# Newton step ahead of a division, two operands on GpSimd, and two more load buffers in a fused attention and feed-forward kernel

## The chip, the core and the metric

The kernel runs on one core of a Trainium2 chip. A core has a matmul engine (TensorE, PE in the profile, whose weight loads are listed apart as PEld), three engines for elementwise work (VectorE or DVE, ScalarE or ACT, GpSimd or POOL) and SyncE (SP), which issues most transfers. Each engine works through its own instructions in the order in which the program gives them, and waits on semaphores for the others. TensorE and ScalarE reach both memories on the chip, SBUF and PSUM; matmul results land in PSUM, and GpSimd does not read them here. The metric is the device time of one execution in microseconds (us); lower is better.

## What is computed

Attention with normalised q and k over 8 batches, 12 heads, 448 positions and 64 features, and behind it a feed-forward block with a softmax-weighted activation and a layer norm. All is float32.

```python
def rmsnorm(x, g):
    return x / np.sqrt(np.mean(x * x, axis=-1, keepdims=True) + 1e-06) * g
scores = scale * np.matmul(rmsnorm(q, g_q), rmsnorm(k, g_k).transpose(0, 1, 3, 2))
attn = np.exp(scores - np.max(scores, axis=-1, keepdims=True))
attn = attn / (np.sum(attn, axis=-1, keepdims=True) + 1e-09)
x = np.matmul(attn, v)                  # brought to (3584, 768)
...
h = x @ w_in                            # (3584, 1024)
e = np.exp(h - np.max(h, axis=-1, keepdims=True))
solu = h * e / (np.sum(e, axis=-1, keepdims=True) + 1e-09)
ln = (solu - mu) / np.sqrt(var + 1e-06) * g_ln
out = ln @ w_out                        # (3584, 768)
```

## The kernel before

Only `fast_path` runs with these inputs. The order of instructions on each engine is written out by hand; three stages follow each other.

**Stage 1, attention** (to about 331 us). A pair n is two heads of one batch; a quad m is two pairs, a = 2m and b = 2m + 1; there are 24 quads. For a pair, `load` (L627) brings q and k in eight transfers on SP's queue (L634) into one tile of the ring `qk`; `squares` (L653, ScalarE), `row_sums` (L660, DVE), `fold_sums` (L668, GpSimd, for a whole quad) and then `rsqrt_seed` (L690, ScalarE: a logarithm and an exponential) and `rsqrt_step` (L697, DVE: one Newton step of four instructions, L701 to L704) make the inverse root of the mean square; `normalise` (L706, GpSimd) multiplies, `qk_transpose` (L720, DVE) turns the result, and `gain` (L725, ScalarE) scales it. This work is for the next quad but one (squares, sums) and the next quad (the rest). For the quad itself `scores` (L804) and `scores_last` make the score blocks on PE and their exponentials E on ScalarE (L802), three PSUM buffers in turn; `add` (L836, DVE) adds two blocks of E into es; `outputs` and `values` (L846, L859) multiply with v into two PSUM banks o, one for each pair; `sums` (L870) adds up E and es on PE. `inverse` (L889) turns those sums round, takes reciprocals (DVE) and copies them between partitions (GpSimd, L903); `divide` (L905) is four DVE instructions (twice L910, L911) that multiply the two banks o by the reciprocals into xo, and so free the banks for the next quad's values; `store_x` (L914) sends xo to DRAM on SP's queue.

`unit` runs one piece and then whatever `later` has put off until then. After quad m's sums, `later(1, divide(m))` makes the division fall due right after the first score block of quad m + 1, ahead of the Newton step for quad m + 2, which in quads 2 and 3 is called after the second and the first score block (L1451 to L1455). SP's order within a quad is: v for the next quad (L647, two more transfers at L651), the store of the quad before, eight q,k transfers for pair a + 6, eight for pair b + 6, and in some quads a piece of w_in (L510).

**Stage 2, first matmul** (to about 585 us). PE multiplies x with w_in in 14 groups of two row tiles by a scheme of seven products instead of eight. A finished tile t goes through `ff_max`, `ff_exp` (ScalarE), `ff_mult` (L1055, a DVE multiply of 128x1024), `ff_moments` (L1059: DVE statistics, and on GpSimd a power, L1071, and a shift, L1073), `ff_norm` (L1075, ScalarE) and `ff_spread` (L1084, a DVE transpose and four stores on SP). The table `waits` in `in_parts` (L1094) says how many units after the tile these five fall due. The last group's tiles are 26 and 27; tile 27 is finished one product ahead of tile 26 and has the key (NG - 1, 1).

**Stage 3, second matmul.** Seven blocks n of four row tiles each, seven products P1 to P7 a block, and seven matmul groups (a "slot" each) a product. `load_u` (L1130) brings the spread tiles back into a ring of six buffers ur (SP, L1133). `make` (L1146) forms the seven operands: a11, a12 and a22 are ScalarE copies (L1151 to L1155), s1, s2, s3, s4 are DVE instructions of 128x512 (L1157 to L1163); s3 of block 0 reads a11 and ur, s4 reads a12 and s2. `inner_sums` (L1165) makes four sums of each operand on GpSimd (L1174 to L1177, 128x256). In `outer_product` (L1179) each slot's result is taken from its PSUM bank by ScalarE or DVE (L1208, L1210, L1235, L1248, L1258), and the next matmul group into that bank waits for this. At the end of `fast_path`, `made(n, name, ...)` puts an operand's two halves behind the slots named; inner sums of a product stand six slots ahead of it. Block 1's loads are put at slots 10, 11, 15 to 18, 21 and 22, its a11 at slots 18 and 21.

Of the kernel before, what the change touches and what calls it, by code (L numbers as in the profile page):

```python
# [9 lines left out]
FP32 = mybir.dt.float32  # L10
# [4 lines left out]
OP = AluOpType  # L15
# [351 lines left out]
def fast_path(  # L367
# [24 lines left out]
    nc = tc.nc  # L392
    B, H, S, D = q.shape
    DM, DFF = moe_w_in.shape
    P = 128
    NJ = S // P
    NB = S // 32
# [6 lines left out]
    NG = NT // 2  # L404
# [14 lines left out]
    loads = first.enter_context(tc.tile_pool(name="loads", bufs=2))  # L419
# [207 lines left out]
    def load(n):  # L627
        b, hp = divmod(n, NP)
        h0 = 2 * hp
        d = st[n] = {}  # L630
        d["qk"] = loads.tile([P, 2, NB, 32], FP32, tag="qk", name="qk", bufs=5)
        for s, src in enumerate((q, k)):
            for g in range(4):
                nc.sync.dma_start(  # L634
                    d["qk"][g * 32 : g * 32 + 32, s],
                    src[b, h0 + g // 2].rearrange("(b t) (x d) -> x t b d", t=32, x=2)[g % 2],
                )
# [162 lines left out]
    def exponentials(d, kc, s):  # L800
        d["E", kc] = big_tile("E")[:, 0 : 2 * S].rearrange("p (h t) -> p h t", h=2)
        nc.scalar.activation(d["E", kc], s[:, :, 0:S], AF.Exp)  # L802

    def scores(n, kc):  # L804
        d = st[n]
        s = ps_t.tile([P, 2, 512], FP32, tag="t", name="s")

        for c in range(0, P, D):
            for h in range(2):
                hh = slice(h * D, (h + 1) * D)  # L810
                keys = slice(NJ * c + kc, NJ * (c + D - 1) + kc + 1, NJ)
                nc.tensor.matmul(  # L812
                    s[c : c + D, h, 0:S], d["qkT"][hh, 1, keys], d["qkT"][hh, 0, :],
                    start=True, stop=True,
                )
        exponentials(d, kc, s)
# [88 lines left out]
    def divide(m):  # L905
        xo = quads[m]["xo"] = work.tile([P, 2, S], FP32, tag="xo", name="xo", bufs=1)
        for i in range(2):
            n = 2 * m + i
            r = work.tile([P, NB, 32], FP32, tag="r", name="r", bufs=1)
            nc.vector.transpose(r, quads[m]["rc"][:, i].rearrange("p t b -> p (t b) ()").to_broadcast([P, NB, 32]))  # L910
            nc.vector.tensor_tensor(xo[:, i], st[n]["o"], r.rearrange("d b i -> d (b i)"), OP.mult)  # L911
            del st[n]

    def store_x(m):  # L914
        b, hp = divmod(2 * m, NP)
        nc.sync.dma_start(
            xd[b].rearrange("(c p) t -> p c t", p=P)[:, hp : hp + 2], quads.pop(m)["xo"]
        )
# [7 lines left out]
    def load_x(g):  # L926
        x = gs[g, "x"] = xs.tile([P, KD, 2 * P], FP32, tag="x", name="xg")
        t = 2 * g * P
        while t < 2 * (g + 1) * P:
            b, c = divmod(t, S)  # L930
            n = min(S - c, 2 * (g + 1) * P - t)
            o = t - 2 * g * P

            (nc.sync if g < 2 else nc.scalar).dma_start(x[:, :, o : o + n], xd[b].rearrange("(c p) t -> p c t", p=P)[:, :, c : c + n])
            t += n

    def sizes(g):

        x = gs[g, "x"].rearrange("p c t -> p (c t)")
        n = HD * 2 * P  # L940
        sm = gs[g, "s"] = xs.tile([P, 3, HD, P], FP32, tag="x", name="xsum")
        for i in range(2):
            nc.scalar.activation(
                sm.rearrange("p k c t -> p (k c t)")[:, 0:n], x[:, i * n : (i + 1) * n], AF.Square,
                accum_out=xmax[:, 2 * g + i : 2 * g + i + 1],
            )
# [7 lines left out]
    def block_sums(g, part):  # L954

        if part == 0:
            gs[g, "A"] = x_blocks(g)
        a11, a12, a21, a22 = gs[g, "A"]
        sm = gs[g, "s"]
        s1, s2, s4 = [sm[:, i] for i in range(3)]  # L960
        if part == 0:
            nc.gpsimd.tensor_tensor(s1, a21, a22, OP.add)
            nc.gpsimd.tensor_tensor(s2, s1, a11, OP.subtract)
        else:
            nc.gpsimd.tensor_tensor(a21, a11, a21, OP.subtract)
            nc.gpsimd.tensor_tensor(s4, a12, s2, OP.subtract)
# [77 lines left out]
    def ff_max(t):  # L1044
        d = mt[t]
        d["nmax"] = small.tile([P, 1], FP32, tag="hmax", name="hmax")
        nc.vector.tensor_scalar(d["nmax"], d["top"], -1.0, None, OP.mult)  # L1047
# [46 lines left out]
    def in_parts():  # L1094
        def done(g, i):
            t = 2 * g + i
            ff_max(t)
            waits = {
                (NG - 2, 1): (1, 2, 3, 5, 5), (NG - 1, 1): (1, 2, 3.25, 6.75, 7), (NG - 1, 0): (2.25, 3.75, 4.75, 7.5, 8)
            }.get((g, i), (1, 2, 3, 5, 7))  # L1100
            for x, f in zip(waits, (ff_exp, ff_mult, ff_moments, ff_norm, ff_spread)):
                later(x, lambda f=f: f(t))

        p = [products(g, lambda i, g=g: done(g, i)) for g in range(NG)]
        parts = [p[0][1], p[0][2]]
        for g in range(NG):
            turn = [p[g][6], p[g][5], p[g][7], p[g][4], p[g][3]]
            x = len(parts)
            if g + 1 < NG:
                turn[3:] = [p[g + 1][1], p[g][4], p[g + 1][2], p[g][3]]  # L1110
            parts += turn
            if g + 1 < NG:
                follow(parts, x, lambda g=g: sizes(g + 1))
                follow(parts, x + 1, lambda g=g: block_sums(g + 1, 0))
                follow(parts, x + 2, lambda g=g: block_sums(g + 1, 1))
            if g + 2 < NG:
                follow(parts, x + 4, lambda g=g: load_x(g + 2))
        return parts
# [9 lines left out]
    us = {}  # L1128
# [6 lines left out]
    def in_turn(n, t, h):  # L1135
        return us[n, "raw", t, h].rearrange("p (a c i) -> p c a i", a=4, c=HF)

    def operand(n, name):
        own = last.get("u", last["first"])
        if (n, name) not in us:  # L1140
            us[n, name] = own.tile(
                [P, 2, HF, 4, 32], FP32, tag="op", name=name, bufs=2 if own is last["first"] else 8
            )
        return us[n, name]

    def make(n, name, t):  # L1146


        o = operand(n, name)[:, t]
        if name == "a11":  # L1150
            nc.scalar.copy(o, in_turn(n, t, 0))  # L1151
        elif name == "a12":
            nc.scalar.copy(o, in_turn(n, t, 1))
        elif name == "a22":
            nc.scalar.copy(o, in_turn(n, 2 + t, 1))  # L1155
        elif name == "s1":
            nc.vector.tensor_tensor(o, in_turn(n, 2 + t, 0), in_turn(n, 2 + t, 1), OP.add)  # L1157
        elif name == "s2":
            nc.vector.tensor_tensor(o, us[n, "s1"][:, t], us[n, "a11"][:, t], OP.subtract)
        elif name == "s3":  # L1160
            nc.vector.tensor_tensor(o, us[n, "a11"][:, t], in_turn(n, 2 + t, 0), OP.subtract)
        else:
            nc.vector.tensor_tensor(o, us[n, "a12"][:, t], us[n, "s2"][:, t], OP.subtract)  # L1163

    def inner_sums(n, name):  # L1165

# [123 lines left out]
    def follow(p, i, f):  # L1290
        g = p[i]

        def both():
            g()
            later(1, f)

        p[i] = both
# [7 lines left out]
    def later(units, f):  # L1305
        todo.append((now + 4 * units, f))

    def unit(f, steps=4):
        nonlocal now
        f()  # L1310
        now += steps
        due = [x for x in todo if x[0] <= now]
        todo[:] = [x for x in todo if x[0] > now]
        for _, g in sorted(due, key=lambda x: x[0]):
            g()
# [40 lines left out]
    with tc.manual_schedule():  # L1356
# [19 lines left out]
        for m in range(NQ):  # L1376
# [7 lines left out]
            next1 = m + 1 < NQ  # L1384
# [48 lines left out]
            def norms_next():  # L1433
                rsqrt_seed(norms[m + 1])
                rsqrt_step(norms[m + 1])
                normalise(a + 2)
                normalise(b + 2)
# [5 lines left out]
            if next1:  # L1443
                load_v(m + 1)
            unit(lambda: scores(a, 0))
            store_x(m - 1)
            if early:
                qk_transpose(a + 2)
                if next3:
                    load(a + 6)  # L1450
            if m == 3:  # L1451
                norms_next()
            unit(lambda: scores(a, 1))
            if m == 2:
                norms_next()  # L1455
            unit(lambda: scores(a, 2))
            if m == 3:
                qk_transpose(a + 2)
# [61 lines left out]
                load_x(1)  # L1520
            unit(lambda: sums(m))
            inverse(m)
            if next1:
                later(1, lambda m=m: divide(m))
            if m == NQ - 2:
                load_x(0)
# [58 lines left out]
        def made(n, name, *slots_of):  # L1585
            for t, slot in enumerate(slots_of):
                when(slot, lambda t=t: make(n, name, t))
# [35 lines left out]
        for x in ("s2", "a12", "s3", "s4", "a22"):  # L1623
            operand(0, x)
        made(0, "s2", 0, 3)
        made(0, "s3", 6, 8)
        made(0, "a12", 10, 11)
        made(0, "a22", 12, 14)
        made(0, "s4", 17, 20)
# [86 lines left out]
```

## Time and profile before

| what | value |
|---|---|
| median of three runs | 822.52 us (819.43 to 822.54) |
| the profiled execution | 824.07 us, its span 821.8 us |
| TensorE matmul busy | 800.8 us, 97% |
| DVE, ScalarE, GpSimd busy | 616.3, 475.3, 469.9 us |
| transfers from SP's queue | 111.8 MB, 52.9% of the time of 16 DMA engines |
| DRAM read and written | 84.9 and 36.7 MB |

A row of a timeline gives the start in us from the span's start, the duration in us, the engine, the line and the operation, what it writes and reads with shapes, how many instructions are merged in it, and in brackets how long the engine was idle before it and what ended that. A row of the table of waits gives the total us, how often, and the longest. In the table by stretch each engine has its busy time and, in brackets, its instructions; then come the granted PE clock (1.00 is full), the busy share of the DMA engines and their GB/s. Starts are nearer the truth than durations on PE: its matmuls overlap, so the listed 0.81 us of a group of four stands for 0.65 us from start to start.

### The profile page before, as it was taken

What the parts mean: (1) busy time and instruction counts of PE and PEld (TensorE: products, weight loads), DVE (VectorE), ACT (ScalarE), POOL (GpSimd) and SP (SyncE); (2) the same over time, 40 slices, a digit from 0 to 9 for tenths busy, and PEclk for the clock granted to TensorE, in tenths of its full rate; (3) what the DMA queues carried; (4) which work ended last, traced back from release to release, by engine and by line L of the source; (5) the groups of instructions that cost most, each with busy time, mean ns of one, the idle gap of its engine ahead of it and who ended that gap; (6) DMA issues with size and microseconds to landing.
All of it is one profiled execution on the core that took longest, in us unless ns stands there. A gap on an engine that the chain in (4) does not pass through costs nothing.

```text
span 821.8 us, 14997 instructions
## 1 busy us (share of the span) xinstructions
PE 800.8 (97%) x5030; PEld 469.7 (57%) x5030; DVE 616.3 (75%) x1217; ACT 475.3 (58%) x785; POOL 469.9 (57%) x635
## 2 busy tenths in 40 slices
PE   8989999999999999999999999999989999999996
PEld 4333444443344443444444444444689999999996
DVE  6867788887878888377878766677786866866945
ACT  6667778776867777366666644444514464464420
POOL 1334546555555647333356467777487777877861
PEclk9999999999999999999999999999999999999999
DMA  6678777877777664235665335453548466376312
GB/s 130 131 146 197 141 187 151 205 148 176 159 175 175 128 158 119 87 103 127 185 166 153 94 95 136 131 143 73 160 122 270 126 211 231 127 243 203 125 59 82
DMA packets 272546, 122.74 MB, mean 149 GB/s; under 512 B 190540, under 2 KB 257612, under 8 KB 272460
## 3 DMA queue, kind: packets, MB, share of 16 engines
q1 hardware_dynamic: 257276, 111.79, 52.9%
q10 hardware_dynamic: 15184, 9.90, 4.5%
q8 instruction: 42, 0.69, 0.4%
q14 instruction: 44, 0.36, 0.2%
HBM read 84.94 MB, written 36.70 MB: 148 GB/s over the span
## 4 chain that ended last, share of the span: by engine, by line
PE 71%; SPq 6%; DMA 5%; DVE 5%; issue 2%; POOL 2%; ACT 1%; DVEq 0%; POOLq 0%; ACTq 0%
PE A L1196 14%; PE A L982 11%; PE B L1196 7%; PE o L865 7%; PE s L812 7%; PE B L982 7%; SPq L634 5%; PE C L982 4%; PE D L982 4%; PE C L1196 4%; PE sm L884 3%; DMA v<-in_v_dram 2%; PE s L825 1%; PE o L854 1%; DMA qk<-in_k_dram 1%
## 5 line engine op out<-in xcount | busy, mean ns | idle before, releaser
L802 ACT ACTIVATE E<-s 128x896 f32<-128x896 f32 x168 | 139.0, 935 | 15.5 <-PE s L812 15.2
L812 PE MATMUL s<-qkT 64*64 64x448 f32 x1152 | 121.1, 547 | 1.5 <-ACT E L802 0.9
L865 PE MATMUL o<-E,v 128*64 128x448 f32 x576 | 113.5, 543 | 0.0
L674 POOL COPY ss<-part 32x56 f32<-32x56 f32 x88 | 42.1, 478 | 97.5 <-DVE part L664 94.8
L713 POOL TENSOR_TENSOR qkn<-qk,ny 128x896 f32<-128x896 f32 x46 | 77.1, 1697 | 27.5 <-DVE ny L704 12.0
L1071 POOL TENSOR_TENSOR he<-he,mhalf 128x1 f32<-128x1 f32 x28 | 27.6, 986 | 105.7 <-DVE he L1070 105.3
L1196 PE MATMUL B<-w_out,sums 128*128 128x192 f32 x392 | 80.4, 328 | 3.3 <-DVE P L1258 2.1
L812 PEld LDWEIGHTS s<-qkT 64*64 64x64 f32 x1152 | 47.7, 163 | 60.7 <-ACT E L802 30.9
L1196 PE MATMUL A<-w_out,sums 128*128 128x192 f32 x392 | 80.6, 329 | 1.0 <-POOL sums L1177 0.7
L865 PEld LDWEIGHTS o<-E,v 128*64 128x64 f32 x576 | 39.2, 137 | 72.7 <-issue 65.2
L982 PE MATMUL B<-w_in,xsum 128*128 128x512 f32 x168 | 76.7, 593 | 0.7 <-POOL he L1071 0.7
L982 PE MATMUL A<-w_in,xg 128*128 128x512 f32 x168 | 74.7, 593 | 0.1
L1196 PEld LDWEIGHTS B<-w_out,sums 128*128 128x128 f32 x392 | 66.9, 191 | 3.9 <-DVE P L1258 2.4
L1053 ACT ACTIVATE u<-h,hmax 128x1024 f32<-128x1024 f32 x28 | 32.2, 1148 | 63.3 <-DVE hmax L1047 63.2
L1196 PEld LDWEIGHTS A<-w_out,sums 128*128 128x128 f32 x392 | 66.8, 191 | 1.7 <-POOL sums L1177 1.6
L982 PEld LDWEIGHTS B<-w_in,xsum 128*128 128x128 f32 x168 | 31.8, 190 | 41.2 <-issue 38.3
L664 DVE TENSOR_REDUCE part<-sq 128x28 f32<-128x896 f32 x46 | 48.6, 1079 | 8.5 <-ACT sq L656 6.5
L982 PEld LDWEIGHTS A<-w_in,xg 128*128 128x128 f32 x168 | 31.8, 190 | 40.5 <-issue 39.1
L723 DVE STREAM_TRANSPOSE qkT<-qkn 128x896 f32<-128x896 f32 x46 | 48.9, 1092 | 6.6 <-POOL qkn L713 6.6
L839 DVE TENSOR_TENSOR es<-E 128x896 f32<-128x896 f32 x48 | 53.3, 1113 | 0.5 <-ACT E L802 0.5
L656 ACT ACTIVATE sq<-qk 128x896 f32<-128x896 f32 x46 | 43.5, 987 | 7.6 <-DMA qk<-in_k_dram 7.3
L563 POOL TENSOR_TENSOR w_out<-w_out 128x384 f32<-128x384 f32 x44 | 45.3, 1036 | 1.3
(151 smaller groups left out, 1625.3 us busy)
## 6 DMA issues: line engine op xcount, KB each, us to landing
ur<-ud SPq DMA_DIRECT2D x60, 256.0 KB, 4.6
ud<-ub SPq DMA_DIRECT2D x112, 128.0 KB, 2.3
xd<-xo SPq DMA_DIRECT2D x24, 448.0 KB, 3.6
qk<-in_q_dram SPq DMA_DIRECT2D x184, 56.0 KB, 2.6
qk<-in_k_dram SPq DMA_DIRECT2D x184, 56.0 KB, 2.4
v<-in_v_dram SPq DMA_DIRECT2D x24, 384.0 KB, 4.4
out_dram<-P SPq DMA_DIRECT2D x19, 384.0 KB, 3.9
raw<-in_moe_w_in_dram SPq DMA_DIRECT2D x12, 512.0 KB, 5.4
```

The lines of the kernel that those rows point to most:

```text
L563: nc.gpsimd.tensor_tensor(o, p, q, OP.subtract)
L656: nc.scalar.activation(d["sq"], d["qk"].rearrange("p s b d -> p (s b) d"), AF.Square)
L664: nc.vector.tensor_reduce(norms[m]["part"][:, i], st[n]["sq"], AX, OP.add)
L674: e.tensor_copy(ss[g * 32 : g * 32 + 32], part[o * 32 : o * 32 + 32])
L713: e.tensor_tensor(d["qkn"], d["qk"].rearrange("p s b d -> p (s b) d"), y.rearrange("p b -> p b ()").to_broadcast([P, 2 * NB, 32]), OP.mult,)
L723: nc.vector.transpose(d["qkT"].rearrange("p s t -> p (s t)"), d["qkn"].rearrange("p b d -> p (b d)"))
L802: nc.scalar.activation(d["E", kc], s[:, :, 0:S], AF.Exp)
L812: nc.tensor.matmul(s[c : c + D, h, 0:S], d["qkT"][hh, 1, keys], d["qkT"][hh, 0, :], start=True, stop=True,)
L839: nc.vector.tensor_tensor(d["es"], d["E", 0], d["E", 1], OP.add)
L865: nc.tensor.matmul(d["o"][h * D : (h + 1) * D, :], quads[n // 2]["v"][:, n % 2 * 2 + h, kc], d["E", kc][:, h], start=False, stop=(kc == NJ ...
L982: nc.tensor.matmul(k[bank], a[:, c], w_in[i][:, c], start=begin and c == 0, stop=c == HD - 1, skip_group_check=not begin,)
L1196: nc.tensor.matmul(k[bank], a[:, c].rearrange("p a i -> p (a i)"), w_out[:, area, i, c], start=begin and c == 0, stop=c == KC - 1, skip_gr ...
```

## The change

- **Quads 2 and 3.** The divisions of quads 1 and 2 are no longer put off with `later`; in quads 2 and 3 they are called behind `norms_next()` (seed, Newton step and the two normalising calls for the next quad). The store of the quad before follows the division.
- **Last stage, first block.** s3 and s4 of block 0 are made by GpSimd. s3 moves from slots 6 and 8 to slots 9 and 10; s4 stays behind slots 17 and 20. The other six blocks keep DVE.
- **Tile 27.** Its `ff_mult` falls due one unit after the tile instead of two.
- **Loads.** The ring for q and k has seven buffers instead of five.

```diff
-        d["qk"] = loads.tile([P, 2, NB, 32], FP32, tag="qk", name="qk", bufs=5)
+        d["qk"] = loads.tile([P, 2, NB, 32], FP32, tag="qk", name="qk", bufs=7)
...
-                (NG - 2, 1): (1, 2, 3, 5, 5), (NG - 1, 1): (1, 2, 3.25, 6.75, 7), (NG - 1, 0): (2.25, 3.75, 4.75, 7.5, 8)
+                (NG - 2, 1): (1, 2, 3, 5, 5), (NG - 1, 1): (1, 1, 3.25, 6.75, 7), (NG - 1, 0): (2.25, 3.75, 4.75, 7.5, 8)
...
-            nc.vector.tensor_tensor(o, us[n, "a11"][:, t], in_turn(n, 2 + t, 0), OP.subtract)
+            (nc.vector if n else nc.gpsimd).tensor_tensor(o, us[n, "a11"][:, t], in_turn(n, 2 + t, 0), OP.subtract)
         else:
-            nc.vector.tensor_tensor(o, us[n, "a12"][:, t], us[n, "s2"][:, t], OP.subtract)
+            (nc.vector if n else nc.gpsimd).tensor_tensor(o, us[n, "a12"][:, t], us[n, "s2"][:, t], OP.subtract)
...
             unit(lambda: scores(a, 0))
-            store_x(m - 1)
+            if m not in (2, 3):
+                store_x(m - 1)
...
             if m == 3:
                 norms_next()
+                divide(m - 1)
+                store_x(m - 1)
             unit(lambda: scores(a, 1))
             if m == 2:
                 norms_next()
+                divide(m - 1)
+                store_x(m - 1)
...
-            if next1:
+            if next1 and m not in (1, 2):
                 later(1, lambda m=m: divide(m))
...
-        made(0, "s3", 6, 8)
+        made(0, "s3", 9, 10)
```

## The prediction

> **What bounds it now.** The page's first part comes first, then the table of TensorE's (PE's) waits, then busy time by stretch.
>
> ```profile
> PE 800.8 (97%) x5030; PEld 469.7 (57%) x5030; DVE 616.3 (75%) x1217; ACT 475.3 (58%) x785; POOL 469.9 (57%) x635
> ```
> ```profile
> PE sm L884 <- DVE es L839: 3.8, 4, 1.9
> PE s L825 <- ACT E L802: 2.7, 3, 1.2
> PE B L1196 <- DVE P L1258: 2.1, 1, 2.1
> ...
> PE B L1196 <- DVE P L1248: 1.2, 1, 1.2
> ```
> ```profile
> 84.00:190.00 106.00, 106.00 (x1064) 44.60 (x1056) 91.37 (x148) 84.04 (x122) 57.66 (x95) 1.00 0.77 173
> 190.00:215.00 25.00, 22.59 (x204) 8.43 (x200) 20.17 (x28) 18.11 (x26) 13.78 (x18) 1.00 0.72 160
> ...
> 567.00:605.00 38.00, 33.99 (x129) 23.34 (x128) 29.16 (x68) 16.45 (x28) 23.55 (x32) 0.96 0.54 155
> ```
>
> PE is the bound; only the 821.8 - 800.8 = 21 us in which it stands, and any time at half clock, can be won. They lie in three places: quads 1 to 4 (26 to 85 us), quad 13 (190 to 215) and the first block of the last stage (585 to 605; its clock column is below 1). The change touches the first and the third. Quads start on PE at 40.66 (2), 55.70 (3), 70.38 (4), 84.65 (5), and then every 12.90 us.
>
> **Early quads: the chain** (timeline, quad 2)
>
> ```profile
> 43.97 0.65 DVE L910 STREAM_TRANSPOSE r<-rc 128x448 f32<-128x448 f32 x1 [1.82 <-POOL rc L903]
> 47.32 0.22 DVE L704 SCALAR_TENSOR_TENSOR ny<-nx,ny 128x56 f32<-128x56 f32 x1
> 47.67 3.35 POOL L713 TENSOR_TENSOR qkn<-qk,ny 128x896 f32<-128x896 f32 x2 [3.74 <-issue]
> 54.05 1.08 DVE L839 TENSOR_TENSOR es<-E 128x896 f32<-128x896 f32 x1
> 55.19 0.59 PE L884 MATMUL sm<-es,ones 128*32 128x224 f32 x8 [1.23 <-DVE es L839]
> ```
>
> VectorE (DVE) idles 1.82 us for GpSimd's copies of rc, divides, and only then takes the Newton step; GpSimd's normalising, two transposes and the sums follow, and PE waits 1.23 us for the last.
>
> **Quad 13: the load queue** (timelines of ScalarE and PE)
>
> ```profile
> 199.35 0.95 ACT L656 ACTIVATE sq<-qk 128x896 f32<-128x896 f32 x1 [3.65 <-DMA qk<-in_k_dram]
> ```
> ```profile
> 202.47 0.59 PE L884 MATMUL sm<-es,ones 128*32 128x224 f32 x8 [1.89 <-DVE es L839]
> ```
>
> ScalarE waits for a q,k load, and es(b) stands behind its square and row sum. The load was late since SP issues back to back from 3.9 to 301 us: 16 q,k issues a quad plus v, store and a weight. SP reaches the v load, its first of a quad, at 87.53 in quad 5 and at 196.96 in quad 13, that is 13.68 us a quad against PE's 12.90. Its lag behind the quad's start on PE grows from 2.9 to 9.0 us, and at 9.0 PE stalls. Quad 12, at 7.8, has es(b) done at 187.30, 0.4 us ahead of need.
>
> **Last stage** (DVE's timeline, then PE's)
>
> ```profile
> 592.04 1.29 DVE L1161 TENSOR_TENSOR s<-a,ur 128x512 f32<-128x512 f32 x2
> ...
> 597.40 0.68 DVE L1163 TENSOR_TENSOR s<-a,s 128x512 f32<-128x512 f32 x1
> ...
> 599.70 0.31 DVE L1258 TENSOR_TENSOR P<-B,u 128x192 f32<-128x192 f32 x1
> ```
> ```profile
> 595.05 0.92 PE L1196 MATMUL B<-w_out,sums 128*128 128x192 f32 x4 [1.16 <-DVE P L1248]
> 600.06 0.92 PE L1196 MATMUL B<-w_out,sums 128*128 128x192 f32 x4 [2.15 <-DVE P L1258]
> ```
>
> DVE has no gap from 585.5 to 601.4; L1248 and L1258 free bank B and stand behind s3, s4 and the last tiles' layer norm. The matmul groups after 600.8 are 1.14 to 1.28 us apart, not 0.65: 3.4 us at half clock, 1.7 us lost.
>
> **Two rules of the Trainium skill.** "TensorE: Matmul & The Clock Gate", Part 1, "What's actually happening": a free-running window of about 3.4 us with too little work halves the clock. The trace agrees in size (3.41 us at half clock after a 2.15 us stall); the 1.89 us stall at 202.47 and the 1.16 us one caused none. I go by these three rows: a stall over about 2 us is dangerous. "SBUF — State Buffer", "Who interferes with whom": a DVE instruction with two SBUF inputs and a GpSimd instruction that reads SBUF exclude each other. The trace agrees: GpSimd's power took 1.46 us beside DVE's 1.22 us multiply at 575.39, but 0.55 at 581.95. So s3 and s4 on GpSimd do not run beside DVE's multiplies and s1 sums; I charge 0.5 us.
>
> **Part by part.**
>
> *Newton ahead of the division, quads 2 and 3.* Nothing is added: four DVE instructions (1.0 us by their starts) go ahead of four (2.65 us); the store keeps its place in SP's order (after the v load, ahead of the q,k loads), and SP arrives at 51.20, past any division time. Quad 2: the seed ends at 43.97, Newton at 44.73 instead of 47.54; es(b) comes at 52.3, before PE needs it: -1.23. The division ends at 47.29 instead of 46.61, and PE's first value matmul, at 46.55, wants that bank: +0.6. The row sums end 2.3 us earlier, so fold and seed no longer stand late in quads 3 and 4. Quad 3: no 0.24 us wait in the sums and no delay around it, -0.5; its division ends 0.3 us later in the quad, with 0.7 us to spare. Quad 4: ScalarE's wait for ss at 72.36 made E late and cost 84.65 - 70.38 - 12.90 = 1.4; all goes. Sum to quad 5: -2.6 us.
> What is late next: SP. PE 2.6 us earlier makes its lag at quad 9 6.7 + 2.6 = 9.3, so PE stalls from there on, and at quad 13 it still waits for the load issued until 196.86. Quad 14 starts at 203.0 as before. On the path I count 0; bounds 0 and -2.6.
>
> *Seven buffers.* A load could wait only for the normalising of the pair five before: SP comes to pair 12's load at 64.0, pair 7 was normalised by 51.0. SP's short stops are for landings. 0. The pool grows by two tiles of 3.5 KB and moves its neighbours; the bound is +-0.3 for the first loads of the next stage.
>
> *s3 and s4 to GpSimd, multiply of the last tile earlier.* DVE loses 1.29 + 0.68 + 0.95 = 2.9 us. The multiply (1.22) now heads DVE's queue while its exponential ends at 585.27, and the last h half (L998), 585.48 before, runs at 586.4: exp of tile 26 one us later, ScalarE's copies behind it too, PE +0.35 once. L1248: 594.65 - 1.29 + 0.2 of gaps = 593.3, so the 1.16 us wait goes. The layer norm of tile 27 is still ahead of L1258: GpSimd's power and shift end at 593.9 (594.6 before), ScalarE's norm at 595.1, its copy u3 (behind operand a11 of block 1) at 596.3, then L1248, transpose 1.2, L1258 at 597.8. Group B starts at 598.15 instead of 600.06: -1.9. That stall is 1.1 us, so the half clock goes: -1.7.
> GpSimd: no row has a 128x512 subtraction there; 128x384 takes 1.00 and 128x256 0.72, so 1.27 each, four of them +5.1. It idles 9.4 us before 592, but in order, behind the power. s3 runs 596.7 to 599.2, sums of a12 600.1 to 603.0, s4 to 605.6, sums of s3 usable at 607.1 + 0.5. Their first reader, P7's third step, was at 609.76; 3.6 earlier it would be at 606.2, so it now waits 1.4. The 0.65 us wait at 613.18 goes with DVE's 3 us lead. Sum at 613: -1.9 - 1.7 + 1.4 (GpSimd) - 0.65 = -2.85. No stall follows until 811 in either. Bounds: -4.0 if GpSimd's lateness is hidden, 0 if half clock stays and the ports cost 1 us.
>
> **Total:** 0 + 0 - 2.85 against the profiled execution's 824.07 (span 821.8 and 2.3 around it) is 821.2. The median of the three runs, 822.52, is 1.55 lower: 819.7.
>
> **Rivals.**
> A (forecast): the early gain is eaten by SP, the last stage gives 2.85: 819.7, own range 817.7 to 821.5. Chance 0.48.
> B: the early gain passes, since SP runs less late without the profiler, or its stops move: one run in three was 3.1 us faster (819.43), as much as quad 13's whole loss (14.99 + 13.85 - 2 x 12.90 = 3.0). 822.52 - 2.85 - 2.6 = 817.1. Against it: SP without a gap in the chain of waits from 115 to 200. Chance 0.25.
> C: GpSimd becomes the bound of the first block and a window of the clock falls in that stall; the gain shrinks to 0 to 1: 822. For it: GpSimd without a gap from 592 to 608 already. Chance 0.17.
> D (slower): block 1's loads take the buffers that s3 reads. In the trace its second and third load start at 592.75 and 593.35, just after DVE's two subtractions end (592.72 and 593.32); the first, at 592.17, waited for neither. If the first now waits for GpSimd's s3 (598.0), it lands 3.3 us after its issue, 601.4; ScalarE's a11 copy waits there, u3 behind it (602.1), DVE's L1248, transpose and L1258 to 603.8. Group B starts at 604.1: +4.0, half clock as before, 826.5. It decides once that load lands after 597.5. Against it: four of six buffers are read by ScalarE copies over by 592. Chance 0.10.
>
> **Chances.** 0.5% is 4.1 us, about what a measurement here tells from no change: under 818.4 is faster, over 826.6 slower. Faster: most of B (0.22) and A's low edge (0.06). Slower: D's upper half and what I have not seen, 0.06. Same: 0.66. The range holds A, B and C: 815.8 to 824.5.
>
> **What would show it.** Right: L704 of quad 2 near 44.5; no es wait in quads 2 and 3; the start of quad 5 near 82; an es wait at quads 9 to 13 that leaves quad 14 near 203; group B of the first block 1 to 2 us after its forerunner; no half clock there. Wrong: quad 14 near 200 (then B), a 3.4 us row of half clock in the last stage (C), or ScalarE waiting for ur around 597 (D).

## The result, and the profile after

The changed kernel takes 825.74 us (median of 20 runs, 821.59 to 828.48) against 822.72 us for the kernel before on the same chip (20 runs): ratio 1.0042, 95% interval [1.0027, 1.0057]. One of these runs of the kernel before took 2163.88 us and is not in the ratio; the other 19 took 818.71 to 824.71 us. The change makes the kernel 3.0 to 3.5 us slower; the prediction had 819.7 us. Rival D happened, the one given a chance of 0.10. Its 826.5 us was 0.8 us from what was measured; its loss of 4.0 us stands against one of some 3.

The first part of the page of the changed kernel, and the largest rows of its waits of PE:

```profile
PE 804.4 (97%) x5030; PEld 467.9 (57%) x5030; DVE 614.5 (74%) x1213; ACT 474.6 (57%) x785; POOL 473.9 (57%) x639
```
```profile
PE A L1196 <- ACT u L1208: 5.2, 1, 5.2
PE s L825 <- ACT E L802: 2.7, 6, 0.6
PE sm L884 <- DVE es L839: 2.3, 3, 1.3
...
PE A L1196 <- POOL sums L1177: 0.8, 1, 0.8
```

The same matmuls, but 804.4 us busy instead of 800.8. Of these 3.6 us, 3.0 lie in stage 1 and 0.7 in stage 3, where time at half clock counts as busy. The two waits for bank B of before (L1258 2.1, L1248 1.2) are gone. In their place stands one of 5.2 us for a copy on ScalarE (L1208, which empties PSUM bank A). The busy times by stretch, with the clock in the third column from the end, say when:

```profile
84.00:190.00 106.00, 104.72 (x1024) 42.13 (x1024) 90.36 (x144) 82.69 (x120) 56.92 (x90) 1.00 0.78 174
190.00:215.00 25.00, 23.20 (x216) 8.63 (x212) 20.24 (x29) 18.41 (x26) 14.14 (x19) 1.00 0.70 149
567.00:605.00 38.00, 32.24 (x114) 19.90 (x113) 25.04 (x59) 15.42 (x29) 23.95 (x31) 0.94 0.44 128
605.00:625.00 20.00, 19.23 (x111) 18.96 (x112) 17.00 (x38) 2.70 (x5) 17.18 (x20) 0.94 0.53 158
```

PE now stands also between 84 and 190 us, where it had not stood at all, and the clock is low on both sides of 605 us: 6.83 us at half clock (600.51 to 607.34) against 3.41 before.

Where the time went, from the two executions (spans 821.8 and 825.8 us, so +4.0): stage 1 ended at 331.51 before and at 333.26 after, +1.75; stage 2 took 0.34 us less; stage 3, from its first to its last matmul, took 230.21 and 233.05 us, **+2.84**; the tail took 0.25 less. The part in stage 1 cannot be put down to the change. Three more executions whose first stage is that of the changed kernel ended it at 327.41, 332.59 and 333.23 us (e1, e9, e3), and e10, whose first stage is that of the kernel before, at 327.52: one look at stage 1 is uncertain by some 6 us, and only the medians can speak of it. Stage 3 repeats much better. In five kernels that have it as before it took 230.21 to 230.23 us with a stretch at half clock (before, e4, e5, e11, e13), and in three more 229.21 or 229.22 us without one (e6, e7, e12). So the 2.84 us are real, 3.8 against an execution without the half clock, and they are most of the result.

The chain of waits of the changed kernel in that stretch (start, us, what; in order of time) names the cause:

```profile
597.41 0.11 POOL sums L1177
597.52 0.57 issue
598.10 1.27 POOL s L1161
599.37 0.02 issue
599.38 2.65 DMA ur<-ud
602.03 0.02 issue
602.06 0.62 ACT a L1151
602.67 0.23 ACT u L1208
602.90 0.02 issue
602.93 0.03 DVE P L1248
...
603.20 1.23 DVE ub L1086
```

GpSimd's first half of s3 ends at 599.37. 10 ns later SP issues the first load of block 1. It lands, ScalarE makes operand a11 from it, then takes the copy u3 (L1208) that stood behind it, then DVE takes L1248, the transpose and L1258. Timelines of SP and ScalarE, before:

```profile
592.17 2.92 SPq L1133 DMA_DIRECT2D ur<-ud  x6
...
595.77 0.60 ACT L1151 COPY a<-ur 128x512 f32<-128x512 f32 x1
596.28 0.31 ACT L1208 COPY u<-A 128x192 f32<-128x192 f32 x1
```

and SP, ScalarE, DVE and PE, after:

```profile
599.38 2.96 SPq L1133 DMA_DIRECT2D ur<-ud  x6
...
602.06 0.62 ACT L1151 COPY a<-ur 128x512 f32<-128x512 f32 x1 [5.51 <-DMA ur<-ud]
602.58 0.31 ACT L1208 COPY u<-A 128x192 f32<-128x192 f32 x1
...
602.93 0.36 DVE L1248 TENSOR_TENSOR P<-B,u 128x192 f32<-128x192 f32 x1 [5.19 <-ACT u L1208]
...
602.95 1.65 PE L1196 MATMUL A<-w_out,s 128*128 128x192 f32 x4 [5.21 <-ACT u L1208]
604.73 1.65 PE L1196 MATMUL B<-w_out,sums 128*128 128x192 f32 x4
```

The load starts 7.2 us later than before, of which 1.4 us are there because stage 3 began later (its first matmul at 586.69 against 585.27). Three engines stop for it: ScalarE for 5.51 us, DVE for 5.19, PE for 5.21. In the program as built, the first load of block 1 took a buffer of the ring ur that an a12 copy of ScalarE had read; after the change it takes one that s3 reads.

The new slots of s3 do not seem to be what hands it over. In e10 below, where s3 stays on DVE at slots 6 and 8 and only tile 27's multiply moves, the first load waits for s3 as well: SP issues it at 588.66, 20 ns after DVE's first half of s3 ends. The table of SP's waits (586 to 603 us) has both halves:

```profile
SPq L1133 <- DVE s L1161: 0.8, 2, 0.6
```

There it costs PE nothing that the trace shows, since DVE makes s3 early. The buffer addresses of two programs that were built but not run point to the engine: with s3 on GpSimd at the old slots 6 and 8, the first load still gets the buffer of s3; with s3 on DVE at slots 9 and 10, it keeps that of a12. By what rule the ring chooses was not followed further.

The early quads did what they were meant to do, and then the gain was gone again. Timelines of DVE and ScalarE, after:

```profile
43.66 0.22 DVE L704 SCALAR_TENSOR_TENSOR ny<-nx,ny 128x56 f32<-128x56 f32 x1
...
79.09 0.95 ACT L656 ACTIVATE sq<-qk 128x896 f32<-128x896 f32 x1 [2.11 <-DMA qk<-in_k_dram]
...
198.79 0.95 ACT L656 ACTIVATE sq<-qk 128x896 f32<-128x896 f32 x1 [2.91 <-DMA qk<-in_k_dram]
```

The last instruction of quad 2's Newton step starts 3.7 us earlier (L704, 47.32 before). Quad 5 starts on PE at 81.09 instead of 84.65; 0.85 of these 3.56 us are there already when quad 2 starts (39.81 against 40.66), so the part itself gave 2.71. ScalarE's squares wait for loads in between and after, and quad 14 starts at 202.43 against 202.99.

### The profile page after: what moved, and what is told of

It reads as the page before. It is cut to its first block, busy times and chain, and to the rows that moved or that the text cites. A ratio compares the mean times of both kernels' runs of the same rounds, so it can differ in the third digit from the quotient of the medians.

```text
span 825.8 us, 14993 instructions
## 1 busy us (share of the span) xinstructions
PE 804.4 (97%) x5030; PEld 467.9 (57%) x5030; DVE 614.5 (74%) x1213; ACT 474.6 (57%) x785; POOL 473.9 (57%) x639
## 4 chain that ended last, share of the span: by engine, by line
PE 69%; SPq 10%; DVE 5%; DMA 5%; ACT 4%; POOL 3%; issue 3%; ACTq 0%; DVEq 0%; POOLq 0%
PE A L1196 14%; PE A L982 13%; SPq L634 8%; PE B L982 8%; PE B L1196 7%; PE o L865 6%; PE s L812 5%; PE C L982 4%; PE D L982 4%; PE C L1196 4%; DMA v<-in_v_dram 2%; PE sm L884 2%; ACT E L802 2%; POOL ss L674 1%; DVE part L664 1%
## 5 line engine op out<-in xcount | busy, mean ns | idle before, releaser
L656 ACT ACTIVATE sq<-qk 128x896 f32<-128x896 f32 x46 | 44.0, 978 | 18.2 <-DMA qk<-in_k_dram 15.8
L1196 PE MATMUL A<-w_out,s 128*128 128x192 f32 x224 | 46.4, 330 | 5.2 <-ACT u L1208 5.2
```

The lines of the kernel that those rows point to most:

```text
L656: nc.scalar.activation(d["sq"], d["qk"].rearrange("p s b d -> p (s b) d"), AF.Square)
L1196: nc.tensor.matmul(k[bank], a[:, c].rearrange("p a i -> p (a i)"), w_out[:, area, i, c], start=begin and c == 0, stop=c == KC - 1, skip_gr ...
```

## Experiments

Each was compared with the kernel before on the same chip; times are medians.

**One part at a time.** First the change without its part in the last stage's operands, and that part alone on the kernel before.

```diff
-            (nc.vector if n else nc.gpsimd).tensor_tensor(o, us[n, "a11"][:, t], ...
+            nc.vector.tensor_tensor(o, us[n, "a11"][:, t], ...
...
-        made(0, "s3", 9, 10)
+        made(0, "s3", 6, 8)
```

> The changed kernel with s3 and s4 of block 0 back on VectorE (s3 behind slots 6 and 8); early quads, seven buffers and the earlier multiply stay. Theory L (block 1's first load takes a buffer that s3 reads, and so waits for GpSimd; about 3 us of the last stage are lost by this alone): 822 to 823.5, as before, and ScalarE's 5.2 us wait before u3 is gone. Theory E (the early part or the seven buffers cost the time, by a slower load queue): 825 or more, and the last stage still as long from its first matmul as in the changed kernel.

> The kernel before with s3 and s4 of block 0 on GpSimd (s3 behind slots 9 and 10) and nothing else. Theory L: 3 us above before (825 to 826.5), the whole loss, with block 1's first load issued when GpSimd ends the first half of s3. Theory E: within 1 us of before.

Measured: e1 822.77 us, ratio 0.9983 [0.9971, 0.9996]; e2 827.90 us, ratio 1.0044 [1.0019, 1.007], somewhat more than Theory L had. The two operands on GpSimd carry the whole loss, 3.7 us by e2 alone. PE and ScalarE in e2:

```profile
602.23 1.65 PE L1196 MATMUL A<-w_out,s 128*128 128x192 f32 x4 [5.11 <-ACT u L1208]
...
601.34 0.62 ACT L1151 COPY a<-ur 128x512 f32<-128x512 f32 x1 [5.41 <-DMA ur<-ud]
```

It is the wait of the changed kernel, with no other part of the change present. Stage 3 took 233.82 us.

**s3 on GpSimd, but written behind the loads.** In the changed kernel s3 moves to slots 13 and 14. The first two loads of block 1 (slots 10, 11) are then written before it and take buffers that ScalarE has read; only the third and the sixth wait for s3.

```diff
-        made(0, "s3", 9, 10)
+        made(0, "s3", 13, 14)
```

> The changed kernel with s3 of block 0 called behind slots 13 and 14 instead of 9 and 10, still on GpSimd; block 1's first two loads then take buffers that ScalarE's a12 copies read, and only the third and sixth wait for s3. Theory L: the 5.2 us wait goes, the first of P6's B groups comes 3 us or more earlier, no half clock there: 820 to 822.5. Theory G (GpSimd's 5 us of added work is the cost, whoever reads the buffer): 825 or more, with TensorE waiting for inner sums.

Measured: 821.15 us, ratio 0.9964 [0.9951, 0.9977], 2.9 us faster than before. Waits of PE in e3:

```profile
PE A L1196 <- DVE u L1210: 1.3, 2, 0.9
PE B L1196 <- DVE P L1258: 1.1, 1, 1.1
```

The 5.2 us wait is gone and so is the half clock; stage 3 took 228.28 us, 1.93 less than before and 4.77 less than the changed kernel. GpSimd does the same work on the same operands, written four slots later; it begins s3 at 598.20, where the changed kernel had 598.10. So it is not the subtraction that costs 5 us, but who waits for it.

About 1.0 of the 1.93 us is the half clock, as the 229.21 us of e6, e7 and e12 show.

**A seventh buffer.** The changed kernel with s3 where the change puts it, and one more buffer in the ring ur for the first load.

```diff
-bufs=2 if own is last["first"] else 6)
+bufs=2 if own is last["first"] else 7)
```

> The whole change, with seven buffers instead of six in the ring ur. Block 1's first load then gets a buffer that nothing has used, so it waits for no engine; its second and third load still wait for GpSimd's two halves of s3. If the wait of that first load is what cost the time: no wait of PE for u L1208 near 600, no 6.8 us at half clock, stage 3 some 3 to 5 us shorter than in the changed kernel, ratio 0.994 to 0.998. If GpSimd's two subtractions are too slow by themselves, or take a port from VectorE: the 5.2 us wait goes, but waits for inner sums or for L1258 take its place and the ratio stays at 1.000 to 1.004.

Measured: 823.17 us, ratio 0.9995 [0.9977, 1.0014]. Both theories have a part in it. Timelines of ScalarE and PE in e9:

```profile
596.15 0.60 ACT L1151 COPY a<-ur 128x512 f32<-128x512 f32 x1
596.66 0.31 ACT L1208 COPY u<-A 128x192 f32<-128x192 f32 x1
602.23 0.62 ACT L1151 COPY a<-ur 128x512 f32<-128x512 f32 x1 [5.26 <-DMA ur<-ud]
...
599.15 0.92 PE L1196 MATMUL B<-w_out,sums 128*128 128x192 f32 x4 [1.06 <-DVE P L1258]
...
607.72 0.89 PE L1196 MATMUL A<-w_out,sums 128*128 128x192 f32 x4 [2.13 <-POOL sums L1174]
```

The first load no longer waits, so u3 is out at 596.66 and group B starts 1.06 us late instead of 5.2. The second load still waits for s3 (ScalarE idles 5.26 us), but by then nothing that PE needs stands behind it. What is late next is GpSimd: 2.13 us for an inner sum. Stage 3 took 229.78 us, 3.27 less than in the changed kernel and 0.43 less than before. The ratio is above the 0.994 to 0.998 that the first theory had. So the wait of the first load is the cause of the loss, shown by two edits that remove it in different ways; GpSimd's own lateness is the second limit, and e3 has less of it (a wait of 0.4 us for sums).

**The other three parts alone.** The early quads (e4), seven buffers for q and k (e7), tile 27's multiply (e10), each on the kernel before.

> The kernel before with the Newton step ahead of the division in quads 2 and 3 and nothing else. Theory S (the load queue eats the gain): quad 5 starts near 82 instead of 84.65, waits for es appear from quad 5 on, quad 14 starts at 203 plus or minus 1, the time is within 1 us of before. Theory P (the gain passes): quad 14 near 200.5, 820 us. Theory E (this part does harm): 824 or more.

> The kernel before with seven buffers for q and k and nothing else. If no load waits for a buffer: within 0.7 us of before, SP's time a quad unchanged. If the two buffers let SP run ahead: 820 or less. If the moved neighbours cost something at the border of the first two stages: 824 or more with a later first matmul of the second stage against the end of quad 23.

> The kernel before with only tile 27's multiply one unit earlier. It moves one VectorE instruction in a queue that has no gap there: both theories of the last stage expect no change, ratio 0.9985 to 1.0015, PE late by up to 0.5 us once at 586. If it is this move that upsets VectorE's order ahead of L1248 and L1258, the waits of group B grow and the ratio is 1.002 or more.

Measured: 823.91 us, 1.0000 [0.9986, 1.0013]; 823.55 us, 0.9991 [0.9976, 1.0006]; 824.96 us, 1.0018 [1.0001, 1.0036]. Quads and buffers are no change. The multiply's interval just leaves 1; but its stage 3 took 230.04 us (230.21 before), its group B waits 2.14 us for L1258 as before, and no wait in its trace is longer. e1, which has the same move, is at 0.9983. I take it as no change, and leave open whether it costs a few tenths of a us. The quads' part did bring quad 5 to 81.34, and quad 14 to 201.53.

**Is it the load queue that eats the early gain?** First the two small loads of v (L651) were moved to ScalarE's queue: in the kernel before (e5), with the early quads' part (e6), and in e3 (e8).

```diff
-            nc.sync.dma_start(d["vl"][i * D : (i + 1) * D], ...
+            nc.scalar.dma_start(d["vl"][i * D : (i + 1) * D], ...
```

> The kernel before with the two short v transfers of a quad (the vl tile, 1.25 us of issue) issued on ScalarE's queue instead of SP's. Theory S (SP's issue rate sets quads 5 to 14): SP needs about 12.4 us a quad, its lag does not grow, the 3 us of quads 13 and 14 go: 819.5 to 821. Rival D (the landings, that is the DMA engines, set the rate, whoever issues): SP still needs 13.3 to 13.7 us a quad, within 1 us of before.

> The same move of the two short v transfers, together with the Newton step ahead of the division in quads 2 and 3. Theory S: the gain of the early quads now passes, 2 to 2.6 us below the kernel with the move alone (817 to 819), quad 14 starts near 197.5. Rival D: no more than 1 us below the kernel with the move alone.

> The changed kernel with s3 behind slots 13 and 14 and the two short v transfers on ScalarE's queue. Theory S and L together: 3 us for the last stage, 3 for quads 13 and 14, 2.6 for the early quads: 815 to 817. Rival D: 819 to 821.5, as with the later s3 alone.

Measured: 862.68, 862.07 and 858.69 us, ratios 1.0464 [1.0434, 1.0495], 1.0440 [1.0401, 1.0479] and 1.0413 [1.0383, 1.0444]. No theory had a loss of 34 to 38 us. ScalarE and PE in e5:

```profile
153.94 1.27 ACTq L651 DMA_DIRECT2D vl<-in_v_dram  x2
155.26 5.78 ACT L802 ACTIVATE E<-s 128x896 f32<-128x896 f32 x7 [1.08 <-PE s L812]
...
156.23 0.98 PE L825 MATMUL s<-qkT 64*64 64x448 f32 x8 [1.71 <-ACT E L802]
```

Two issues take 1.27 us on ScalarE, ahead of the exponentials that PE waits for: 30.6 us of such waits (19 times) where the kernel before has 2.7, most of the loss. But SP did not get ahead either. Its own waits in e5 have a row that the kernel before does not have:

```profile
SPq L634 <- DMA vl<-in_v_dram: 44.4, 32, 8.0
```

The q,k issues on SP now wait for the loads of v that ScalarE issues late, SP needs 15.13 us a quad (quads 5 to 13), and the squares wait 30.2 us for q,k. Which of the two, the issues on ScalarE or SP's waits, makes the exponentials late is not separated. The queue was not relieved, so these three runs decide nothing between the theories.

Next the loads were left out from quad 2 on, in the kernel before (e11) and with the early quads' part (e12). These two kernels multiply with old rows of v, so their output is wrong; only their time is of use.

```diff
-        d["vl"] = loads.tile([P, 2, D], FP32, tag="vl", name="vl", bufs=2)
+        d["vl"] = loads.tile([P, 2, D], FP32, tag="vl", name="vl", bufs=2) if m < 2 else quads[m - 2]["vl"]
...
-        for i in range(2):
+        for i in range(2 if m < 2 else 0):
```

> The kernel before without the two small loads of v (L651) from quad 2 on; the quads then use the rows that quads 0 and 1 loaded. SP has two issues, 1.26 us, less in each quad and no other engine has more. If SP's issue rate bounds quads 5 to 13: 12.4 us a quad for SP, less than PE's 12.9, its lag at quad 13 below 5 us, no wait for es in quad 13 and none in ScalarE for a q,k load; start of quad 14 near 200, stage 1 some 2.5 to 4 us shorter, ratio 0.995 to 0.997. If SP's pace is set by how soon its transfers land and not by their number: SP stays near 13.5 us a quad and the ratio at 0.9985 to 1.001.

> The same with the early quads' part of the change. If SP's queue had eaten their gain of 3.5 us: quad 5 near 81, quad 14 near 197, and 2.5 to 3.5 us less than the run without that part, ratio 0.991 to 0.9935. If something else than SP takes the gain back: within 1 us of that run.

Measured: 819.72 us, 0.9950 [0.9937, 0.9964], and 817.13 us, 0.9943 [0.9918, 0.9969], the second a little short of its 0.991 to 0.9935. In the trace of e11 PE has no stop from 84 to 330 us (windows), and ScalarE's squares hardly wait, 0.7 us in all (groups by line; 7.6 before and 18.2 in the changed kernel):

```profile
84.00:190.00 106.00, 106.00 (x1060) 44.88 (x1056) 92.17 (x150) 84.24 (x121) 58.58 (x95) 1.00 0.78 172
190.00:330.00 140.00, 140.00 (x1354) 58.04 (x1347) 115.80 (x176) 99.73 (x143) 82.82 (x123) 1.00 0.62 141
```
```profile
L656 ACT ACTIVATE sq<-qk 128x896 f32<-128x896 f32 x46 | 42.8, 994 | 0.7 <-DMA qk<-in_k_dram 0.7
```

That trace alone proves nothing. e10 has the first stage of the kernel before, with all its loads, and its one trace, of the fastest of 22 runs, has no stop either (the same two stretches):

```profile
84.00:190.00 106.00, 106.00 (x1056) 44.88 (x1060) 92.13 (x150) 84.02 (x122) 58.38 (x95) 1.00 0.79 176
190.00:330.00 140.00, 140.00 (x1354) 58.64 (x1351) 116.43 (x176) 100.08 (x143) 82.88 (x123) 1.00 0.65 147
```

So the load queue stops PE in some executions and not in others, and it is the medians that show what it costs: 819.72 against 824.08 us. With these loads left out, the early gain comes through: the median falls by another 2.6 us, where the same edit with the loads in place is worth nothing (e4, 1.0000). The intervals of e11 and e12 overlap, but 8 of the 11 runs of e12 are below the fastest of the 22 runs of e11 (817.81 us). The traces agree: quad 5 at 81.12 and quad 14 at 197.28 against 83.68 and 199.75, both 2.5 us earlier.

What in the queue it is, the number of issues or the transfers, was tried with the same loads on GpSimd's queue: in the kernel before (e13) and in e3 (e14). And e3 without the early quads' part (e15).

```diff
-            nc.sync.dma_start(d["vl"][i * D : (i + 1) * D], ...
+            nc.gpsimd.dma_start(d["vl"][i * D : (i + 1) * D], ...
```

> The kernel before with the two small loads of v (L651) issued on GpSimd's queue: the same bytes, two issues a quad less on SP. If the number of SP's issues sets its pace: as without those loads, SP near 13.0 us a quad, ratio 0.994 to 0.998. If the transfers set it: 1.000. If an issue on GpSimd costs what it cost on ScalarE, but on an engine that has 43% idle: no more than 1.003; if it costs several us each, or its writes hold VectorE up, GpSimd's normalising comes late, PE waits for scores and the ratio is above 1.01.

> The changed kernel with s3 at slots 13 and 14, and the same two loads on GpSimd's queue. If the number of issues holds the early quads' gain: 0.988 to 0.992, some 4 to 6 us below e3 less what GpSimd's issues cost. If not: within 0.002 of e3 (0.9964), or above it by what e13 loses.

> The changed kernel with s3 at slots 13 and 14 and without the early quads' part. If that part is worth nothing on the path: as e3, 0.995 to 0.998, the last stage near 228.3 us. If e3's gain came partly from the early quads: 0.998 to 1.000.

Measured: e13 823.40 us, 0.9990 [0.9969, 1.0011]; e14 817.95 us, **0.9907 [0.9884, 0.993]** (6 runs, 814.6 to 818.33); e15 822.80 us, 0.9978 [0.9966, 0.9989]. SP's pace in single traces decides nothing: from quad 6's v load to quad 14's it is 13.68 us a quad before, 13.60 in e13 and 13.05 in e11, but also 13.10 in e10, with every load on SP. By the medians, two issues less on SP gained nothing that can be told from noise (e13), while leaving the loads out altogether gained 0.5% (e11); the intervals do not touch. SP in e13:

```profile
115.19 2.97 SPq L634 DMA_DIRECT2D qk<-in_q_dram  x4
118.20 3.96 SPq L634 DMA_DIRECT2D qk<-in_k_dram  x4
122.26 1.98 SPq L634 DMA_DIRECT2D qk<-in_q_dram  x4
```

The same four issues take 1.98 us or twice that; the long ones follow the v load and the store. The page "DMA: Bandwidth & Descriptors" of the Trainium skill, section "Issuing engines are not separate DMA queues", says that transfers of all issuing engines run on the same 16 DMA engines and that another issuing engine saves only the sequencer's time. e13 agrees. e14 does not follow from it: it is the fastest version that computes the right output, 4.7 us under e3 by the ratios, as the theory of the number of issues had it, while the same move is worth nothing in e13. In its one trace the squares wait 7.1 us for loads, against 13.5 us in e3. So that these loads take the early gain is shown; whether by their number or by their transfers, and why the move pays only in e14, stays open.

e15 has 228.26 us in stage 3, so the last stage without the bad wait is worth 0.22% (1.8 us), as its 1.95 us less in the trace say. The step to e3 (1.2 us) is what the early quads may add; the intervals overlap.

## Why the prediction was wrong, point by point

- **Newton ahead of the division: -2.6 us to quad 5, 0 on the path.** Right. From the start of quad 2 to that of quad 5 PE needs 43.99 to 44.25 us in seven kernels without the part (before, e2, e7, e10, e11, e13, e15) and 41.28 to 41.53 in seven with it (after, e1, e3, e4, e9, e12, e14): 2.7 us. (The listed terms add to -2.5.) On the path it is worth nothing (e4, 1.0000), and that the loads take it back is shown by e11 and e12. That quad 14, foretold near 203.0, came at 202.43 is luck: in e1, with the same first stage, it came at 199.85. Imprecise was how: stops were foretold from quad 9 on, in the changed kernel the first came in quad 5 (95.16 - 81.09 = 14.07 us to the next, not 12.90).
- **Seven buffers: 0.** Right, 0.9991 [0.9976, 1.0006].
- **GpSimd 1.27 us for each half of s3 and s4.** Right: 2.48 us for two. Its start was right too. s3 began at 598.10 instead of 596.7, but stage 3 had begun 1.42 us later; counted from its first matmul, 11.41 us against 11.43.
- **Last stage -2.85 us.** Wrong by sign. The step that failed is one sentence of rival D: "four of six buffers are read by ScalarE copies over by 592". With it D got a chance of 0.10, and the wait of block 1's first load was left out of the sum. It counted who reads the six buffers, and not which of them the ring hands to the first load once s3 is on GpSimd: in the changed kernel it is the one that the first half of s3 reads. So the load waited for GpSimd until 599.38, and PE stood 5.21 us for the copy u3 behind it, where the sum had group B (the matmuls into bank B) 1.9 us earlier and no half clock. Stage 3 became 2.84 us longer. The point of decision ("once that load lands after 597.5") was right: it landed near 602.0.
- **The terms of -2.85, with that wait away.** e3 shows them. Group B stalls 1.06 us (foretold 1.1), and counted from the first matmul of stage 3 it starts 2.0 us earlier than before (foretold 1.9). There is no half clock (foretold), but that was put at 1.7 us and is worth 1.0 (230.21 us of stage 3 with it, 229.21 without). New waits are 0.9 us for L1210 and 0.4 for sums in this block, together near the foretold 1.4, which was all to be for sums. Stage 3 is 1.93 us shorter, so two thirds of the sum came, and most of the rest is the half clock.
- **Rival D's 826.5.** The path was right, the +4.0 us too much: stage 3 lost 2.84, the medians differ by 3.0. The load landed 2.65 us after its issue, not 3.3. PE stopped one group earlier than D had it, at bank A for u3 (602.95); group B at 604.73 (foretold 604.1, with stage 3 beginning 1.42 us earlier) then waited for nothing. The half clock was to be "as before" and was twice that, with 2.44 of the 6.83 us in the stall itself; what it cost here is not separated. That D's time came within 0.8 us is in part luck.
- **The range, 815.8 to 824.5,** did not reach D because its chance was put at 0.10. The trace of before had the sign to weigh it more: the second and third load started within 40 ns of the ends of DVE's two s3 halves. Loads already waited on s3; the change made s3 later and reordered who waits.

## What to carry to other kernels

When an operation moves to a slower engine or a later slot, look up the next user of every buffer that it reads, not only the reader of what it writes: here a subtraction of 1.24 us on an engine with 43% idle cost more than 5 us on each of three others, through a load that nobody had moved. Which buffer a ring hands out can change when a reader changes its engine, and even when an instruction moves that does not touch the ring (e10), so the lateness of a reader can fall on another load. With s3 written behind the two urgent loads, the changed kernel gained 2.9 us instead of losing 3. And a gain upstream of a queue that already runs late must be costed at that queue, by medians of many runs where single traces of one program differ by 6 us.

## What the hardware showed that was not expected

A stall of the same length halves the clock in one execution and not in the next. In each trace the edges of the granted clock lie on a grid of 3.413 us (600.95 and 819.40 in the kernel before are 64 steps apart). Stretches on that grid for the kernel before (first two rows) and for e1 (two rows), the clock third from the end:

```profile
597.54:600.95 3.41, 1.26 (x8) 0.97 (x7) 3.41 (x7) 1.56 (x2) 3.15 (x5) 1.00 0.28 98
600.95:604.36 3.41, 3.41 (x13) 3.41 (x12) 1.54 (x5) 0.00 (x0) 3.33 (x6) 0.50 0.89 247
```
```profile
590.41:593.82 3.41, 2.87 (x16) 2.57 (x16) 3.24 (x10) 2.52 (x5) 3.17 (x5) 1.00 1.02 351
593.82:597.23 3.41, 1.54 (x9) 1.34 (x9) 3.23 (x7) 1.37 (x2) 3.23 (x6) 1.00 0.38 107
```

Both have a stall of 2.15 us. Before, it lies whole in one cell of the grid, and the next cell is at half clock; in e1 it is split 0.28 and 1.87 and nothing happens. In stage 3 this holds in every trace with such a stall: 2.14 to 2.16 us inside one cell gave 3.41 us at half clock (before, e4, e5, e10, e11, e13), no more than 1.87 in any one cell gave none (e1, e6, e7, e9, e12). In the changed kernel two cells with 2.77 and 2.44 us of the stall were each followed by one at half clock. In stage 1 of e5, 2.04 us in one cell (77.97 to 81.38) were enough. A cell that is itself at half clock was kept there by less: 0.93 us without a busy PE in e2, 1.75 and 1.54 in e5 and e6, while 0.70 in e8 let it go. Idle time does not explain all: near 9 us, ahead of the first quad, cells with 1.90 (e6) and 1.65 us (e8) were followed by half clock.

The page "TensorE: Matmul & The Clock Gate" of the Trainium skill (Part 1, "What's actually happening") has the free-running window of 3413 ns, which these edges agree with. Its advice to leave no idle gaps over about 3 us ("Why this matters for your kernels") is too mild for this case, where 2.04 us in one window were enough. A slow window cost stage 3 1.0 us, and whether it comes is a matter of phase, which any edit far upstream shifts: it belongs in a range, not in a sum.
